# A bounce through memory issued on another queue, and weight loads put behind a cast, in an attention and Fourier-mix kernel on one core

## The chip, the cores and the metric

The kernel runs on one core of one Trainium2 chip. A core has a matrix engine (TensorE, PE in the profile; PEld is its loading of weights), a vector engine (VectorE, DVE), a scalar engine (ScalarE, ACT), GpSimd (POOL), a synchronisation engine (SyncE, SP) that here only issues transfers, and 16 DMA engines. Each engine works through its own list of instructions in order, and a transfer is issued by an instruction in the list of SP, ACT or POOL. The metric is the device time of one execution in microseconds (us); lower is better.

## The reference

Batch 4, 8 heads, 768 positions, head size 64. Attention keeps a local band of 96 positions and the first 8 positions, with a linear distance bias; its output goes through a two-dimensional Fourier transform, and a two-layer block with a residual follows.

```python
scores = scale * np.matmul(q, k.transpose(0, 1, 3, 2))
scores = scores + bias[None, :, :, :]
scores = np.where(keep, scores, -1000000000.0)      # band of 96, and the first 8
a = softmax(scores);  x = heads_joined(a @ v)        # 4 x 768 x 512
mixed = np.real(np.fft.fft(np.fft.fft(x, axis=1), axis=2))
u = x + mixed
un = (u - mu) / np.sqrt(var + 1e-06)
out = u + np.maximum(un @ w_ch1, 0.0) @ w_ch2        # 512 -> 2048 -> 512
```

## The kernel before

Each batch b goes through the same stages. Loads of q, k, v for one pair of heads at a time (hp 0 to 3) come in on SP (`run_dma`, L365; `load`, L320). They are cast to 16 bits (`cast_qk`, L369 on ACT and L373 on POOL; v in `cast_v0`, L414 on POOL), transposed (`trans`, pt, L515, copied to qkT by L521 on DVE or L525 on ACT), and multiplied to scores (`score`, sc, L542 to L552). ACT takes the exponential into ex (L575). A few global columns go their own way (`glob`, pgl and eg; `v_global`, pvg and vG). `v_place` (pvp, L427) puts v into its place. `av` (pav, L669 and L680) multiplies by v, and DVE divides the result into X, the tile x of a batch (L699, L700).

X is then used twice. DVE folds it (L797 to L819), PE makes the first Fourier stage y (py, L881, copied to zy by L896 on ACT and L898 on DVE) and, with mirrored copies made on POOL (L916 to L929), the second one (`u_unit`, pu, L961). Beside that, `bounce(b)` (L709) writes X to a scratch tensor xd in memory (L719) and reads it back into xr in the other order of rows that the Fourier output has (L727). `u_unit` adds the two on DVE: u = pu + xr (L980). From there come the normalised un (L995 on ACT, L997 on DVE), its transpose ptu and unT (L1025, L1033, L1035), the sum of squares (L1004), the hidden layer ph (L1053, 8 units for each of the 12 pieces c of 256 rows, three pieces to a batch; evacuated to hT by L1059 on ACT or L1060 on DVE), and the output layer pg (L1076), whose result is added to u (L1085) and stored (L1090).

The two weight matrices are 4 MB each in 32 bits. `wload` (L1159) loads and casts them in eight transfers, four of w_ch1 (L1164) and four of w_ch2 (L1169), all issued by POOL. They go into the buffers that staged q and k of batch 1. `hold` (L1178), a tiny transfer on SP, waits for the last of them; it is the gate (`("gate",)`) behind which the loads of batch 2 stand.

The order on every engine is fixed when the program is built. A planner (class `Plan`) keeps a clock for each engine and for the DMA, and gives each piece of work to the engine and place where it would end first by its estimates; `later` (L61) registers a piece with its needs, its cost on the engine and, as `dma=`, the time its transfer takes. So a changed need or cost can move many other instructions.

For batch 0 the bounce writes two halves, heads 0 to 3 and heads 4 to 7, as four transfers of 192 KB on SP; for the other batches it writes two of 384 KB on ACT. The transfers issued by SP and ACT signal their end on eight semaphores, DMAHW0 to DMAHW7, taken in turn in the program's order, and an issue that takes one again waits until the earlier transfer on it has landed.

Of the kernel before, what the change touches and what calls it, by code (L numbers as in the profile page):

```python
# [176 lines left out]
def kernel(  # L177
# [11 lines left out]
    nc = tc.nc  # L189
# [94 lines left out]
    def free(tag, i):  # L284
        i -= NBUF[tag]
        return [("free", tag, i)] if i >= 0 else []

    def buf(tag, i, shape, dtype, users):
        pl.users(("free", tag, i), users)
        return wk.tile(shape, dtype, tag=tag, name=f"{tag}_{i}", bufs=NBUF[tag])  # L290
# [417 lines left out]

    def bounce(b):  # L709

        on, eng = ("ACT", nc.scalar) if b else ("SP", nc.sync)
        parts = ((0, 256), (256, 512)) if b == 0 else ((0, Dm),)
        for n, (c0, c1) in enumerate(parts):
            def wr(n=n, c0=c0, c1=c1):
                if n == 0:
                    XD[b] = dr.tile([S, Dm], FP16, tag="xd", name=f"xd_{b}", bufs=2)
                rows = XD[b][:, c0:c1].rearrange("(j m t) d -> t m j d", t=2, m=64)
                for t in range(2):
                    eng.dma_start(rows[t], X[b][64 * t:64 * t + 64, :, c0:c1])  # L719
            pl.later([(on, 1.2, wr)], [("x", b, hp, jp) for hp in range(c0 // P, c1 // P) for jp in range(NP)]  # L720
                     + [("xw", b, n - 1)] * (n > 0), 0.0, [("xw", b, n)], [("free",) + XT[b]] * (3 - len(parts)),
                     lat=1.7, dma=2.4 / len(parts))

        def rd():
            XR[b] = buf("xr", b, [P, NS, Dm], FP16, 3)
            rows = XD[b].rearrange("(m r) d -> m r d", r=6)
            eng.dma_start(XR[b], rows)  # L727
        pl.later([(on, 0.5, rd)], [("xw", b, n) for n in range(len(parts))] + free("xr", b), 0.0, [("xr", b)], lat=1.7, dma=3.8 if b else 2.4)
# [369 lines left out]
    with tc.manual_schedule():  # L1098
# [60 lines left out]
        def wload(i):  # L1159
            a = i % 4  # L1160
            if i < 4:
                if i == 0:
                    W1[0] = buf("w1", 1, [P, ND, 4 * Dm], FP16, 1)
                nc.gpsimd.dma_start(W1[0][:, :, a * 512:(a + 1) * 512],  # L1164
                                    moe_w_ch1[:, a * 512:(a + 1) * 512].rearrange("(c p) f -> p c f", p=P))
            else:
                if i == 4:
                    W2[0] = buf("w2", 1, [P, NJ, Dm], FP16, 1)
                nc.gpsimd.dma_start(W2[0][:, 4 * a:4 * a + 4, :],  # L1169
                                    moe_w_ch2[a * 512:(a + 1) * 512, :].rearrange("(c p) f -> p c f", p=P))  # L1170
        for i in range(8):
            needs = [("ld", 7, 1), ("free", "w1", 0)] if i == 0 else [("wl", 3), ("free", "w2", 0)] if i == 4 else [("wl", i - 1)]
            pl.later([("POOL", 0.85, lambda i=i: wload(i))], needs, 0.0,
                     [("w1" if i < 4 else "w2", i % 4)], lat=2.2, dma=3.3, rank=0,
                     then=lambda t, i=i: pl.tok.__setitem__(("wl", i), pl.t["POOL"]))
# [4 lines left out]
        for b in range(B):  # L1180
# [36 lines left out]
            else:  # L1217
# [12 lines left out]
                for half in range(2):  # L1230
                    for jp in range(NP):
                        av(b, (2 * half, 2 * half + 1), jp)
            bounce(b)
            if b < DB:
                fold_3(b)
# [53 lines left out]
```

## Time and profile before

| | before |
|---|---|
| time, median of 3 runs | 287.69 us (286.93 to 289.57) |
| the profiled execution: own time, span in the profile | 288.64 us, 286.9 us |
| PE busy | 258.0 us, 90% |
| PE weight loads, DVE, ACT, POOL busy | 173.3, 153.9, 150.1, 55.9 us |
| mean granted clock of PE, share of full speed | 0.969 |
| queue of SP | 31.40 MB, 44.8% of 16 engines' span |
| queue of POOL (the weights) | 4.19 MB, 8.7% |
| queue of ACT | 4.72 MB, 6.6% |

The profile is one execution. Busy shares are means over the span. The profile's chain of the work that ended last lists what the last instruction goes back to; the waits name, for each engine, whose result it waited for. A transfer's time to landing runs from the start of its issue to its last byte.

### The profile page before, as it was taken

To read this page: it belongs to the slowest core of one execution; us is meant where nothing else is said; L and a number is where in the kernel's file an instruction comes from. 1 tells how busy PE (TensorE), PEld (TensorE's weight loads), DVE (VectorE), ACT (ScalarE), POOL (GpSimd) and SP (SyncE) were. 2 spreads that over 40 slices of the span, in tenths; PEclk is the share of its full clock that TensorE was granted. 3 is DMA by queue.
4 is the path that set the end of the run, shared out by engine and by line. 5 is a ranking of instruction groups with operands and counts; after the bars stand their busy time and mean duration, and the time that the engine had idled before them with its cause. 6 is when DMAs were issued, how large, how long until landed. Compare 5 with 4: busy or idle time off the path is not lost.

```text
span 286.9 us, 6013 instructions
## 1 busy us (share of the span) xinstructions
PE 258.0 (90%) x2448; PEld 173.3 (60%) x2448; DVE 153.9 (54%) x323; ACT 150.1 (52%) x256; POOL 55.9 (19%) x126
## 2 busy tenths in 40 slices
PE   1898994048999999999999999999999999999994
PEld 1354574017778785578558466677677567777441
DVE  4557930057039952669268969666995552211121
ACT  1489772028875962578684144979044155534000
POOL 1442496001121042130311024201002211100000
PEclk9999999557999999999999999999999999999999
DMA  7999999997005895795696897400073020100211
GB/s 218 289 292 315 317 239 217 223 228 169 3 10 158 156 250 114 199 224 125 125 235 161 162 248 180 94 13 2 2 172 124 37 75 1 39 37 0 75 73 73
DMA packets 70301, 40.69 MB, mean 142 GB/s; under 512 B 27394, under 2 KB 66306, under 8 KB 70274
## 3 DMA queue, kind: packets, MB, share of 16 engines
q1 hardware_dynamic: 63218, 31.40, 44.8%
q0 software_dynamic: 4224, 4.19, 8.7%
q10 hardware_dynamic: 2832, 4.72, 6.6%
q8 instruction: 19, 0.31, 0.5%
q14 instruction: 8, 0.07, 0.1%
HBM read 31.92 MB, written 9.44 MB: 144 GB/s over the span
## 4 chain that ended last, share of the span: by engine, by line
PE 69%; SPq 2%; POOL 1%; DMA 1%; DVE 1%; issue 1%; DVEq 0%; POOLq 0%
PE ph L1053 29%; PE pg L1076 26%; PE py L881 3%; PE pav L680 3%; PE sc L552 3%; PE pu L961 2%; PE ptu L1025 2%; SPq L494 1%; PE pav L669 1%; DMA out_dram<-u 1%; POOL ww L929 1%; PE pgl L632 1%; DVE u L980 0%; SPq L336 0%; POOL v L454 0%
## 5 line engine op out<-in xcount | busy, mean ns | idle before, releaser
L1053 PE MATMUL ph<-unT,w 128*128 128x256 f16 x768 | 93.7, 273 | 0.5 <-ACT v L444 0.5
L1076 PE MATMUL pg<-w,hT 128*128 128x512 f16 x384 | 89.3, 379 | 0.0
L1053 PEld LDWEIGHTS <-w 128*128 128x128 f16 x768 | 72.5, 98 | 16.4 <-issue 4.7
L1059 ACT ACTIVATE hT<-ph 128x512 f16<-128x512 f32 x76 | 45.3, 596 | 44.9 <-PE ph L1053 44.4
L1076 PEld LDWEIGHTS <-hT 128*128 128x128 f16 x384 | 36.8, 98 | 37.1 <-issue 0.4
L1085 DVE SCALAR_TENSOR_TENSOR u<-pg,sm,u 128x512 f32<-128x512 f32 x24 | 18.0, 748 | 45.7 <-PE pg L1076 45.5
L980 DVE SCALAR_TENSOR_TENSOR u<-pu,xr 128x512 f32<-128x512 f32 x24 | 15.6, 686 | 22.2 <-DMA xr<-xd 15.3
L575 ACT ACTIVATE ex<-sc 128x992 f16<-128x992 f32 (+2 forms) x24 | 21.1, 926 | 10.2 <-PE sc L552 9.9
L572 ACT ACTIVATE er<-sc 128x992 f16<-128x992 f32 (+2 forms) x24 | 21.7, 922 | 6.1 <-PE sc L552 5.2
L995 ACT ACTIVATE un<-u,sm 128x512 f16<-128x512 f32 x10 | 7.2, 719 | 27.0 <-DVE sm L984 27.0
L1060 DVE TENSOR_SCALAR hT<-ph 128x512 f16<-128x512 f32 x20 | 13.8, 691 | 10.2 <-PE ph L1053 10.0
L542 PE MATMUL sc<-dist,sid 128*128 128x480 f16 x16 | 5.4, 426 | 15.0 <-DVE u L980 15.0
L929 POOL COPY ww<-zy 128x512 f16<-128x512 f16 x16 | 9.4, 614 | 44.9 <-PE py L881 44.9
L552 PE MATMUL sc<-qkT 64*128 64x256 f16 (+1 forms) x192 | 17.5, 269 | 0.5 <-DVE qkT L521 0.5
L1011 POOL TENSOR_SCALAR sm<-sm 128x2 f32<-128x2 f32 x12 | 2.3, 193 | 75.8 <-ACT un L1004 75.6
L680 PE MATMUL pav<-v,ex 128*128 128x65 f16 x352 | 16.2, 193 | 0.7 <-DVE x L700 0.7
L1035 DVE COPY unT<-ptu 128x1024 f16<-128x1024 f16 x10 | 6.9, 688 | 17.7 <-PE ph L1053 15.0
L680 PEld LDWEIGHTS <-ex 128*128 128x128 f16 x352 | 15.0, 97 | 2.0 <-DVE x L700 0.9
L896 ACT ACTIVATE zy<-py 128x1024 f16<-128x1024 f32 (+1 forms) x10 | 8.6, 856 | 14.2 <-PE py L881 14.1
L587 DVE TENSOR_TENSOR ex<-er,mk 128x992 f16<-128x992 f16 (+2 forms) x24 | 15.0, 641 | 1.7 <-ACT er L572 1.7
L369 ACT ACTIVATE qk<-qs 128x384 f16<-128x384 f32 (+1 forms) x29 | 13.6, 526 | 4.6 <-DMA qkT<-qk 4.6
L1004 ACT ACTIVATE un<-un 128x512 f16<-128x512 f16 x24 | 14.8, 621 | 1.6 <-PE ptu L1025 1.6
(102 smaller groups left out, 304.3 us busy)
## 6 DMA issues: line engine op xcount, KB each, us to landing
out_dram<-u SPq DMA_DIRECT2D x24, 256.0 KB, 2.1
w<-in_moe_w_ch_dram POOLq DMA_DIRECT2D x8, 512.0 KB, 16.2
qs<-in_q_dram SPq DMA_DIRECT2D x9, 384.0 KB, 4.1
qs<-in_k_dram SPq DMA_DIRECT2D x9, 384.0 KB, 4.3
u<-in_v_dram SPq DMA_DIRECT2D x8, 384.0 KB, 7.1
qs<-in_v_dram SPq DMA_DIRECT2D x16, 192.0 KB, 3.9
xr<-xd ACTq DMA_DIRECT2D x3, 768.0 KB, 5.0
w<-in_q_dram SPq DMA_DIRECT2D x4, 384.0 KB, 7.1
```

The source lines that it names most:

```text
L552: nc.tensor.matmul(pa[:, s, c0:c0 + cw], TT[n][lo:lo + 64, 1, i * P:(i + 1) * P], TT[n][lo:lo + 64, 0, i * P:i * P + cw], start=(b > 1), s ...
L572: A(mine(), cut(pa), AF.Exp, 0.0, 0.125)
L575: A(cut(expst[hp][:, :, g * 512:g * 512 + (384 if g == 2 else 512)]), cut(pa), AF.Exp, 0.0, 0.125)
L587: VT(o, mine(), m, op=ALU.mult)
L680: nc.tensor.matmul(po[:, jj, hh * 65:(hh + 1) * 65], lhsT, v16[b % 2][:, i, h, 0:65], start=(jp == 0 and a == 0), stop=(a == len(ops) - 1) ...
L980: V.scalar_tensor_tensor(u[:, a].rearrange("p (n r) -> p n r", r=4), pu[:, a].rearrange("p (r n) -> p n r", r=4), 1.0, XR[b][:, rr].rearra ...
L1004: A(x, x, AF.Square, accum_out=MV[c][:, a, 2:3])
L1053: nc.tensor.matmul(ph[:, a * CH:(a + 1) * CH], W1[0][:, d, jb * P:(jb + 1) * P], UNT[c][:, d, :], start=(d == 0), stop=(d == ND - 1))
L1059: pl.later([("ACT", act(512), lambda: A(dst, ph, AF.Relu)), ("DVE", dve(512), lambda: V.tensor_scalar_max(dst, ph, 0.0))], [], e, [("h", c ...
L1060: ("DVE", dve(512), lambda: V.tensor_scalar_max(dst, ph, 0.0))],
L1076: nc.tensor.matmul(pg, HT[c][:, jb, t * P:(t + 1) * P], W2[0][:, jb, :], start=(jb == 0), stop=(jb == NJ - 1))
L1085: V.scalar_tensor_tensor(UT[c][:, t, :], pg, MV[c][:, t, 3:4], UT[c][:, t, :], op0=ALU.mult, op1=ALU.add)
```

## The change

Two edits, and an estimate that goes with the first. The bounce of batch 0 is issued in ACT's list, writes and read, where it stood in SP's. The planner's estimate for each of its two writes goes from 1.2 to 2.6 us. The first weight load needs ("vc", 5), the cast of v of batch 1's second pair of heads on POOL, where it needed the landing of the last k of batch 1, ("ld", 7, 1).

```diff
     def bounce(b):
-        on, eng = ("ACT", nc.scalar) if b else ("SP", nc.sync)
+        on, eng = "ACT", nc.scalar
         parts = ((0, 256), (256, 512)) if b == 0 else ((0, Dm),)
...
-                     lat=1.7, dma=2.4 / len(parts))
+                     lat=1.7, dma=2.4 if b else 2.6)
...
         for i in range(8):
-            needs = [("ld", 7, 1), ("free", "w1", 0)] if i == 0 else [("wl", 3), ("free", "w2", 0)] if i == 4 else [("wl", i - 1)]
+            needs = [("vc", 5), ("free", "w1", 0)] if i == 0 else [("wl", 3), ("free", "w2", 0)] if i == 4 else [("wl", i - 1)]
```

The planner then orders anew. ACT's list of before, from the place where the first half of X of batch 0 is done (ex_81 and ex_78 are exponentials, qk_455 to qk_669 casts of batch 1's q and k, qkT_678 a transpose's copy):

```order
L444 ACTIVATE v_82<-pvp_442 128x3x2x64 [waits PE_49]
L369 ACTIVATE qk_455<-w_0_163 128x768 [waits DMAHW0_49]
L575 ACTIVATE ex_81<-sc_0_461 128x2x496 [waits PE_49]
L369 ACTIVATE qk_498<-w_0_163 128x768 [waits DMAHW1_49,Activation_49,Pool_49]
L575 ACTIVATE ex_81<-sc_1_474 128x2x2x240 [waits PE_49]
L575 ACTIVATE ex_81<-sc_2_485 128x2x384 [waits PE_49]
L645 ACTIVATE eg<-pgl_1_501,gb 32x512 [waits PE_49]
L369 ACTIVATE qk_581<-w_0_215 128x768 [waits DMAHW4_49,PE_49,Activation_49]
L575 ACTIVATE ex_78<-sc_0_597 128x2x496 [waits PE_49]
L575 ACTIVATE ex_78<-sc_1_610 128x2x2x240 [waits PE_49]
```

The same place after:

```order
L444 ACTIVATE v_82<-pvp_442 128x3x2x64 [waits PE_49]
L719 DMA xd_471<-x_368 64x6x256 [waits DVE_49]
L719 DMA xd_471<-x_368 64x6x256 [waits DMAHW1_49]
L575 ACTIVATE ex_81<-sc_0_461 128x2x496 [waits PE_49]
L575 ACTIVATE ex_81<-sc_1_474 128x2x2x240 [waits PE_49]
L575 ACTIVATE ex_81<-sc_2_485 128x2x384 [waits PE_49]
L645 ACTIVATE eg<-pgl_1_502,gb 32x512 [waits PE_49]
L369 ACTIVATE qk_591<-w_0_215 128x768 [waits PE_49,DMAHW4_49,Activation_49,Pool_49]
L575 ACTIVATE ex_78<-sc_0_597 128x2x496 [waits PE_49]
L719 DMA xd_471<-x_368 64x6x256 [waits DMAHW0_49,DVE_49]
L719 DMA xd_471<-x_368 64x6x256 [waits DMAHW1_49]
L575 ACTIVATE ex_78<-sc_1_627 128x2x2x240 [waits PE_49]
```

The four writes now stand between exponentials, three of them behind a semaphore of an earlier transfer, and two casts have left this stretch of ACT for POOL; the read L727 follows seven rows later, behind the last exponential into ex_79 and ahead of the first copy of y, and one more cast and the copy qkT_678 have left ACT by then, the copy for DVE.

POOL's list of before, from the third transpose of batch 1 (kG are small copies, er casts of v of batch 1):

```order
L481 COPY kG_85<-qkT_646 64x8 x2
L1164 DMA w_1_689<-in_moe_w_ch_dram 128x4x512
L481 COPY kG_85<-qkT_678 64x8
L1164 DMA w_1_689<-in_moe_w_ch_dram 128x4x512
L481 COPY kG_85<-qkT_678 64x8
L1164 DMA w_1_689<-in_moe_w_ch_dram 128x4x512 x2
L414 CAST er_755<-u_257 128x768
L1169 DMA w_1_760<-in_moe_w_ch_dram 128x4x512
L414 CAST er_762<-u_271 128x768
L1169 DMA w_1_760<-in_moe_w_ch_dram 128x4x512 x3
```

The same place after:

```order
L481 COPY kG_85<-qkT_645 64x8 x2
L373 CAST qk_668<-w_0_215 128x768
L481 COPY kG_85<-qkT_685 64x8 x2
L414 CAST er_732<-u_257 128x768
L414 CAST er_763<-u_271 128x768
L1164 DMA w_1_765<-in_moe_w_ch_dram 128x4x512 x4
L929 COPY ww_818<-zy_759 128x512
L1169 DMA w_1_833<-in_moe_w_ch_dram 128x4x512
L916 COPY rev_0_853<-zy_759 128x2
L917 COPY rev_0_853<-zy_759 128x2x127
L918 COPY rev_0_853<-zy_759 128x256
L1169 DMA w_1_833<-in_moe_w_ch_dram 128x4x512
```

All eight weight loads now come behind both casts, and the four of w_ch2 stand between the mirrored copies of batch 0.

ACT's list of before, ahead of the first hidden unit (hT from ph_0; ex_81 is batch 1's last pair of heads here):

```order
L1004 ACTIVATE un_917,sm_888<-un_917 128x512 x2
L1059 ACTIVATE hT_1017<-ph_0_1022 128x512
L609 ACTIVATE vG_87<-pvg_0_1050 32x4x64 x2
L1059 ACTIVATE hT_1017<-ph_1_1059 128x512
L1059 ACTIVATE hT_1017<-ph_2_1070 128x512
L645 ACTIVATE eg<-pgl_0_1080,gb 64x512
L1059 ACTIVATE hT_1017<-ph_3_1086 128x512
L1059 ACTIVATE hT_1017<-ph_4_1096 128x512
L575 ACTIVATE ex_81<-sc_0_1106 128x2x496
```

The same place after:

```order
L575 ACTIVATE ex_81<-sc_0_961 128x2x496
L575 ACTIVATE ex_81<-sc_1_983 128x2x2x240
L575 ACTIVATE ex_81<-sc_2_994 128x2x384
L444 ACTIVATE v_83<-pvp_1003 128x3x2x64
L1004 ACTIVATE un_953,sm_901<-un_953 128x512 x2
L645 ACTIVATE eg<-pgl_0_1039,gb 64x512
L609 ACTIVATE vG_87<-pvg_0_1050 32x4x64
L995 ACTIVATE un_1079<-u_1044,sm_1045 128x512
L609 ACTIVATE vG_87<-pvg_0_1050 32x4x64
L1059 ACTIVATE hT_1102<-ph_0_1107 128x512
```

Batch 1's last three exponentials, eg and vG, which stood between hidden units, now come ahead of the first of them; on PE the scores, pgl, pvg and two pav units move with them.

## Rows read from the trace of the kernel before

**Rows 1.** The page: PE's busy tenths in 40 slices of 7.17 us.
```profile
PE   1898994048999999999999999999999999999994
```
**Rows 2.** The waits of PE: total us, times, longest.
```profile
PE sc L542 <- DVE u L980: 15.0, 1, 15.0
```
**Rows 3.** Timeline of DVE: start, us, instruction, idle before it and its releaser.
```profile
22.93 0.69 DVE L700 TENSOR_TENSOR x<-pav,rc 128x512 f16<-128x512 f32 x1
...
30.86 0.42 DVE L700 TENSOR_TENSOR x<-pav,rc 128x256 f16<-128x256 f32 x1
...
60.25 0.69 DVE L980 SCALAR_TENSOR_TENSOR u<-pu,xr 128x512 f32<-128x512 f32 x1 [15.31 <-DMA xr<-xd]
```
**Rows 4.** Timeline of SP's list.
```profile
17.65 2.24 SPq L365 DMA_DIRECT2D w<-in_q_dram  x1
...
25.65 0.43 SPq L365 DMA_DIRECT2D w<-in_q_dram  x1
...
35.41 3.96 SPq L719 DMA_DIRECT2D xd<-x  x4
53.38 0.35 SPq L727 DMA_DIRECT2D xr<-xd  x1
65.67 0.32 SPq L1178 DMA_DIRECT2D hold<-w  x1
```
**Rows 5.** Issues: KB each, median us to landing; the third row of 38 to 39.5 us alone.
```profile
w<-in_q_dram SPq DMA_DIRECT2D x4, 384.0 KB, 7.1
...
xr<-xd SPq DMA_DIRECT2D x1, 768.0 KB, 6.7
...
xd<-x SPq DMA_DIRECT2D x2, 192.0 KB, 13.5
...
xd<-x ACTq DMA_DIRECT2D x4, 384.0 KB, 4.6
...
xr<-xd ACTq DMA_DIRECT2D x3, 768.0 KB, 5.0
```
**Rows 6.** Queues from 46 to 50 us: packets, MB, share of 16 engines.
```profile
q0 software_dynamic: 573, 0.57, 83.7%
q1 hardware_dynamic: 572, 0.28, 34.9%
```
**Rows 7.** Timeline of POOL.
```profile
34.84 0.95 POOL L1164 DMA_DIRECT2D w<-in_moe_w_ch_dram  x1
...
40.14 0.83 POOL L414 CAST er<-u 128x768 f16<-128x768 f32 x1
```
**Rows 8.** Timelines of ACT, its exponentials and its issues, and of PE's first pu.
```profile
36.47 3.45 ACT L575 ACTIVATE ex<-sc 128x992 f16<-128x992 f32 x4
...
89.36 1.34 ACTq L719 DMA_DIRECT2D xd<-hT  x2
...
44.07 1.06 PE L961 MATMUL pu<-t,zy 128*128 128x128 f16 x16
```
**Rows 9.** Stretches: length, busy us (instructions) of PE, PEld, DVE, ACT, POOL, clock, DMA share, GB/s.
```profile
60.25:70.57 10.32, 8.07 (x92) 5.19 (x93) 8.74 (x24) 6.77 (x13) 0.92 (x2) 0.63 0.84 174
...
61.61:67.90 6.29, 6.29 (x61) 3.67 (x62) 4.78 (x13) 4.71 (x9) 0.36 (x2) 0.50 0.60 113
...
70.57:117.90 47.33, 47.33 (x450) 34.43 (x449) 24.38 (x48) 30.89 (x57) 8.86 (x20) 1.00 0.55 118
118.14:282.96 164.82, 164.72 (x1424) 110.50 (x1424) 93.57 (x182) 82.04 (x147) 21.59 (x53) 1.00 0.42 103
```
**Rows 10.** The six stretches, 72.05 to 85.94 us, of batch 1's scores, pvg, pgl and two pav.
```profile
sum 4.01, PE 4.01 PEld 1.99 DVE 0.99 ACT 3.34 POOL 0.42; mean PE 0.67 PEld 0.33 DVE 0.17 ACT 0.56 POOL 0.07
```
**Rows 11.** Groups of ACT from 61.7 to 83.4 us: busy, mean ns, idle before.
```profile
L575 ACT ACTIVATE ex<-sc 128x960 f16<-128x960 f32 (+2 forms) x5 | 4.5, 909 | 1.1 <-PE sc L552 0.9
...
L609 ACT ACTIVATE vG<-pvg 32x256 f16<-32x256 f32 x2 | 0.7, 374 | 0.1
L645 ACT ACTIVATE eg<-pgl,gb 64x512 f16<-64x512 f32 x1 | 0.7, 683 | 0.0
```

## The prediction

> **What bounds the kernel now.** I read the slices of the page first. PE is busy nearly all through, but for the start and for three slices near 50 to 65 us, the 0 among them [rows 1]. The waits give that hole one cause: PE stands 15.0 us, once, for the addition u on DVE [rows 2]. DVE's timeline carries it on: u had been idle 15.31 us and was released by the landing of xr, at 60.25 us [rows 3]. So the hole is the bounce of batch 0, and SP's timeline shows where the bounce loses its time. The first half of X is complete when L700 ends at 22.93 + 0.69 = 23.62 us and the second at 31.28 [rows 3], but SP issues the four writes from 35.41 on, behind its loads, 11.8 us after the first half is there, and the read only at 53.38 [rows 4]. The last writes took 13.5 us to land [rows 5], because POOL had begun to issue the weights at 34.84 [rows 7]: between 46 and 50 us the weights' queue and SP's moved the same number of packets, 573 and 572, but the weights' are twice as large and hold 83.7% of the engines' time [rows 6]. From 70.57 us to the last matmul at 282.96, PE is busy all the time except 0.33 us [rows 9] (0.23 between the two stretches, 0.10 in the second). So whatever brings the first hidden unit ph_0 forward brings the end forward by as much, until PE finds a new wait.
>
> A second loss hangs on the hole: when PE resumes, the granted clock is 0.50, the 1.2 GHz level, for 6.29 us of full work [rows 9]. That is up to 3.1 us, but DVE is busy 8.74 of the 10.32 us of that stage too, so I don't take it as a gain of its own.
>
> **The change, part by part.** I follow the time of four events: the read's landing, u, ph_0, the end.
>
> *Bounce on ACT.* Its first write goes out at 23.7. A pair of write issues costs ACT 1.34 us [rows 8], and the second write waits for DMAHW1, which in the program's order is the load issued at 17.65; a load lands 7.1 us after its issue [rows 5], so 24.8. ACT is free again at 25.5 to 25.7, and what is queued behind it, the exponential that before began at 24.36, is 1.3 us late. Two casts that stood in this stretch are now POOL's, so the following eg is only 0.6 late, and X's second half is done at 31.9 instead of 31.28. The second pair waits for the load issued at 25.65, which lands at 32.75, and say 33.3 since the first writes share its engines. ACT is free at 33.3 + 1.34 = 34.65; the exponential behind it is 2.9 late. A cast and a qkT copy have left the list before the read (0.84 and 1.44, given back), and three exponentials at 3.45 / 4 = 0.86 us each [rows 8] lead up to it, so ACT comes to the read at about 39.7, against 39.05 for the same place before. For the landing of the writes I take ACT's other ones, 4.6 us [rows 5], not SP's 13.5, since no weight is under way: 34.65 + 4.6 = 39.3. So ACT hardly waits. The read takes 5.0 us (ACT's) to 6.7 us (SP's, beside the weights) [rows 5]: it lands at 44.8 to 46.7.
>
> *What ACT's lateness costs.* The late exponentials free their PSUM banks later, so y starts some 1.5 us later, and pu_0, which ended at 45.1 (44.07 + 1.06 [rows 8]), ends near 46.6. This is my estimate from the 2.9 us less what is given back; bounds 0 and 3 us. u therefore starts at **46.8**, where both come together, against 60.25. Bounds: 45.1 (no lateness at all) and 50.5 (the second writes land in 8.8 us, half way between the two rows).
>
> *From u to ph_0.* Before, this took 10.32 us with ACT busy 6.77 [rows 9]. After, more stands ahead of ph_0: three exponentials, eg and two vG copies are new and one exponential has moved out, 2 x 0.909 + 0.683 + 0.748 = 3.25 us [rows 11], which makes 10.0 us for ACT, the busiest engine (DVE 8.74 + 0.99 [rows 9, 10]). un starts some 1.5 us after u, and about 1 us of waits between ACT, PE and DVE will remain, about what L575 alone waited before, 1.1 [rows 11]. Together 12.5 us: ph_0 at **59.3**. Bounds 11 and 14.
>
> *From ph_0 to the end.* Before, 282.96 - 70.57 = 212.39 us, less 0.33 idle. The scores, pvg, pgl and two pav that stand ahead of ph_0 now are 4.01 us of PE [rows 10]. Left are 208.05. PE then ends at 267.4, and the tail after the last matmul, 286.9 - 282.96 = 3.94, is untouched: 271.3.
>
> *Weights later.* The first is issued behind the cast er of the second pair. That ran at 40.14 before, after weight issues [rows 7]; now its v load, delayed by the writes that share the engines, sets it, and I take the same 40.1 and 0.83 us. The first issue moves from 34.84 to about 41.0, 6.2 us. From the first issue to hold, which waits for the last weight, it was 65.67 - 34.84 = 30.8 us [rows 4, 7], beside 0.79 MB of writes, 0.79 MB of read and the end of the loads. After, the first writes are gone from it, but batch 1's writes come into it. So hold goes at 71.8. PE wants the last quarter of w_ch1 seven units into the hidden layer, near 66, and half of 30.8 puts it at 56.4. It wants the last quarter of w_ch2 near 76, 4 us after hold. ACT wants the first q of batch 2, behind the gate, near 77, when that has just landed. What hides the delay is thus the stage from u to ph_0 and nine units of work; the cover is 4 us for pg and about none for the cast. For that wait, and for batch 1's writes beside the last weights, I add 1.0 us, bounds 0 and 4.
>
> Sum: 271.3 + 1.0 = 272.3 of span, 14.6 less than 286.9. The profiled execution took 288.64 us, 1.74 outside its span, and the median of the runs is 287.69, 0.95 lower; taking the same 14.6 off the median gives **273.1**.
>
> Against this change speaks the Trainium skill, DMA: Bandwidth & Descriptors, section "Issuing engines are not separate DMA queues": transfers run on the same 16 engines whoever issues them, and another issuer saves only the issuer's time, usually small. By that rule the edit of the queue would be worth next to nothing, the last rival below. The trace disagrees on "small" for this list (the 11.8 us above) and agrees that no bytes are saved, the first rival.
>
> **Rivals.**
> *The wait moves to the weights.* The bytes are the same, so what the bounce no longer waits, the weights do. If hold comes at 77 instead of 71.8, pg of the first piece and the cast of batch 2's q, both in order on engines that PE needs, stand 4 to 5 us: 278. For it: batch 1's writes now fall into the last weights. Against: the 30.8 us already held as many foreign bytes.
>
> *The bounce is still slow.* The second writes land in 13.5 us as SP's did: 48.2. ACT stands at the read from 39.7 with the copies of y behind it, PE stops, the read lands at 55, u starts 8.5 us later than I say and the clock falls as before (up to 3): 283. For it: the loads fill the engines until about 40. Against: ACT's writes of other batches, 4.6.
>
> *Slower than before.* The gate alone could do that. It must hold batch 2's first q 14.6 us longer than I say, hold at 86 or later, so the weights would need 45 us instead of 30.8; decisive from there on. Nothing in the trace slows them so: with the bounce beside them they held 83.7% [rows 6].
>
> *It doesn't do what it says.* If PE, freed at 46.8, lacked work until weights came, 13 us would be lost again: no change. Against: ten us of ACT and nine of PE work stand ahead of ph_0, and w_ch1's first quarter needs only a quarter of 15.4 us after 41.
>
> **How the numbers follow.** My sum 0.70, with its own range 269.5 to 276.5; the weights 0.17; the slow bounce 0.08; no change 0.02; slower 0.03. Low end: u at 45.1, 11 us to ph_0, no wait: 45.1 + 11 + 208.05 + 3.94 = 268.1, which is 268.9 on the median; all at once is unlikely, so 269.5. High end: 50.5, 12.5, waits of 3 give 278.0, which is 278.8; with the weights' 278 inside I close at 279.5. A measurement tells about 1% (2.9 us) from no change. Faster by over 1%: 0.70 + 0.17 + 0.08 = 0.95; same 0.02; slower 0.03.
>
> **What would show it.** Right: the writes on ACT's queue from about 24 and 33 us; the read landing by 47; no PE wait of over 3 us near 50, and a granted clock at 2.4 GHz throughout; ph_0 near 59; hold near 72; PE without gaps after it. Wrong: an ACT wait of several us at L727 before 48 (slow bounce); PE waiting at pg for w, or ACT at L369 for qs, near 75 (weights); ph_0 later than 62 with ACT idle in between (my 12.5 is off).

## Result, and the profile after

The changed kernel takes **279.8 us** (median of 4 runs, 278.83 to 280.46), the kernel before beside it 288.32 (286.93 to 289.57): a ratio of 0.970 (95% interval 0.9645 to 0.9761). The gain is 8.5 us; the prediction said 14.6 and a range up to 279.5. One further run of the same kernel gave 278.78 us and a further series of four 279.03, both below. The profiled execution took 280.46 us, the longest of its four; its span is 278.7. The ratios, but not the medians and ranges, leave out slow runs, those over 1.5% longer than the fastest of their kernel, such as the 283.47 us further down.

From the page, PE's busy tenths and its clock in 40 slices, where [rows 1] had the hole:

```profile
PE   1999789598789999999999999999999999999994
PEclk9999999999999999999999999999999999999999
```

The waits of PE (total us, times, longest). The 15.0 us for u of [rows 2] are gone. The longest behind the start are now one for un and two for hT:

```profile
PE ptu L1025 <- ACT un L995: 2.5, 1, 2.5
PE ph L1053 <- DVE hT L1060: 2.2, 2, 1.4
```

Timelines of the engines (start, us, instruction, idle before it), for the rows that answer to [rows 3, 4, 7]:

```profile
25.99 0.69 DVE L700 TENSOR_TENSOR x<-pav,rc 128x512 f16<-128x512 f32 x1
...
26.71 1.88 ACTq L719 DMA_DIRECT2D xd<-x  x2
...
34.98 1.26 ACTq L719 DMA_DIRECT2D xd<-x  x2
...
41.61 0.35 ACTq L727 DMA_DIRECT2D xr<-xd  x1
...
42.67 3.19 POOL L1164 DMA_DIRECT2D w<-in_moe_w_ch_dram  x4
...
49.81 0.69 DVE L980 SCALAR_TENSOR_TENSOR u<-pu,xr 128x512 f32<-128x512 f32 x1 [0.29 <-PE pu L961]
...
51.16 2.78 DVE L984 TENSOR_SCALAR sm<-sm 128x2 f32<-128x2 f32 x1
...
53.98 0.72 ACT L995 ACTIVATE un<-u,sm 128x512 f16<-128x512 f32 x1 [3.05 <-DVE v L443]
...
64.33 1.03 PE L1053 MATMUL ph<-unT,w 128*128 128x256 f16 x8
...
69.54 0.31 SPq L1178 DMA_DIRECT2D hold<-w  x1
```

The issues (KB each, median us to landing), against [rows 5]:

```profile
xd<-x ACTq DMA_DIRECT2D x4, 192.0 KB, 6.4
xr<-xd ACTq DMA_DIRECT2D x1, 768.0 KB, 4.3
```

The two stretches from u to ph_0 and behind it (columns as in [rows 9]):

```profile
49.81:64.33 14.52, 10.35 (x186) 6.86 (x179) 12.88 (x28) 11.19 (x23) 9.29 (x18) 1.00 1.24 206
64.33:118.00 53.67, 51.05 (x465) 37.81 (x462) 29.68 (x59) 29.78 (x58) 11.30 (x23) 1.00 0.74 164
```

The bounce goes as the change says. In this profile u no longer waits for xr at all: the read landed at 41.61 + 4.3 = 45.9, and u waited for pu. Yet u comes at 49.81 instead of 46.8, ph_0 14.52 us later instead of 12.5, and from ph_0 to the end it is 278.7 - 64.33 = 214.4 us instead of 213.0. In this last stretch PE has 53.67 - 51.05 = 2.62 us of idle instead of 1.0; its work and the tail together came out 0.2 us shorter. These three terms make the span 3.0 + 2.0 + 1.4 = 6.4 us longer than the 272.3 predicted. The experiments ask where each comes from.

### The profile page after: what moved, and what is told of

Same layout as the page of the kernel before. It is cut to its first block, busy times and chain, and to the rows that moved or that the text cites. A ratio compares the mean times of both kernels' runs of the same rounds, so it can differ in the third digit from the quotient of the medians.

```text
span 278.7 us, 6005 instructions
## 1 busy us (share of the span) xinstructions
PE 258.7 (93%) x2448; PEld 173.2 (62%) x2448; DVE 157.9 (57%) x323; ACT 148.0 (53%) x255; POOL 60.8 (22%) x127
## 2 busy tenths in 40 slices
DMA packets 70301, 40.69 MB, mean 146 GB/s; under 512 B 27394, under 2 KB 66306, under 8 KB 70274
## 3 DMA queue, kind: packets, MB, share of 16 engines
q10 hardware_dynamic: 4576, 6.29, 8.3%
## 4 chain that ended last, share of the span: by engine, by line
PE 81%; DVE 8%; ACT 4%; issue 2%; DMA 2%; POOL 1%; ACTq 1%; SPq 0%; DVEq 0%; POOLq 0%
PE pg L1076 29%; PE ph L1053 29%; PE py L881 5%; PE sc L552 4%; PE pav L680 3%; PE pu L961 3%; ACT ex L575 2%; PE pt L515 2%; DVE qkT L521 2%; PE ptu L1025 2%; DMA ident<-idm 2%; PE sc L547 2%; PE pav L669 1%; PE sc L542 1%; DVE sm L984 1%
## 5 line engine op out<-in xcount | busy, mean ns | idle before, releaser
L1059 ACT ACTIVATE hT<-ph 128x512 f16<-128x512 f32 x73 | 43.6, 597 | 48.1 <-PE ph L1053 46.9
L1060 DVE TENSOR_SCALAR hT<-ph 128x512 f16<-128x512 f32 x23 | 15.9, 690 | 11.5 <-PE ph L1053 11.5
L1011 POOL TENSOR_SCALAR sm<-sm 128x2 f32<-128x2 f32 x12 | 3.2, 264 | 71.9 <-ACT un L1004 71.7
L980 DVE SCALAR_TENSOR_TENSOR u<-pu,xr 128x512 f32<-128x512 f32 x24 | 15.6, 688 | 4.7 <-PE pu L961 4.0
L369 ACT ACTIVATE qk<-qs 128x384 f16<-128x384 f32 (+1 forms) x31 | 14.5, 528 | 6.1 <-DMA qkT<-qk 4.8
L995 ACT ACTIVATE un<-u,sm 128x512 f16<-128x512 f32 x12 | 8.5, 716 | 16.1 <-DVE sm L984 13.0
L552 PEld LDWEIGHTS <-qkT 64*128 64x128 f16 x192 | 6.0, 96 | 16.1 <-issue 13.2
L896 ACT ACTIVATE zy<-py 128x512 f16<-128x512 f32 (+1 forms) x10 | 8.1, 810 | 14.7 <-PE py L881 14.7
L898 DVE CAST zy<-py 128x512 f16<-128x512 f32 (+1 forms) x9 | 8.3, 927 | 10.5 <-ACT zy L896 6.4
```

The lines of the kernel that those rows point to most:

```text
L552: nc.tensor.matmul(pa[:, s, c0:c0 + cw], TT[n][lo:lo + 64, 1, i * P:(i + 1) * P], TT[n][lo:lo + 64, 0, i * P:i * P + cw], start=(b > 1), s ...
L980: V.scalar_tensor_tensor(u[:, a].rearrange("p (n r) -> p n r", r=4), pu[:, a].rearrange("p (r n) -> p n r", r=4), 1.0, XR[b][:, rr].rearra ...
L1059: pl.later([("ACT", act(512), lambda: A(dst, ph, AF.Relu)), ("DVE", dve(512), lambda: V.tensor_scalar_max(dst, ph, 0.0))], [], e, [("h", c ...
L1060: ("DVE", dve(512), lambda: V.tensor_scalar_max(dst, ph, 0.0))],
```

## Experiments

**Both kernels once more.** No edit.

> The kernel before once more, for a second profile of its start. Theory (the start varies by itself): PE's slow first matmuls last a different time from run to run, so the third L700, which ended at 23.62 us in the first profile, may end anywhere from 23 to 27 us, and the end does not follow it, since the addition u waits for the read anyway and starts at 60 us within 0.5. Rival (the start is fixed by the program, and the change moved it): it ends at 23.6 within 0.3 again.

> The changed kernel once more. Theory (the start varies by itself, and nothing hides it any more): the third L700 ends between 23 and 27 us, and u starts 23.1 us after that end, as in its first profile (49.81 after 26.68), so an early start is an early end. DVE's L984 at u takes over 2 us again, in a stretch where POOL is busy without a gap. Rival: L700 ends at 26.7 within 0.3 again.

Measured: 287.11 and 278.78 us, spans 285.3 and 277.0. The start of a run varies. Before, the first half of X was ready at 23.62 [rows 3]; in the second profile of the same kernel at 26.23, 2.6 us later, and it costs nothing, because DVE's idle time ahead of u shrinks from 15.31 to 11.16 us. u itself came 1.7 us earlier (I had said within 0.5), as the read was issued earlier, at 51.70 instead of 53.38:

```profile
25.54 0.69 DVE L700 TENSOR_TENSOR x<-pav,rc 128x512 f16<-128x512 f32 x1
...
58.55 0.69 DVE L980 SCALAR_TENSOR_TENSOR u<-pu,xr 128x512 f32<-128x512 f32 x1 [11.16 <-DMA xr<-xd]
```

The changed kernel's second profile had the early start (24.12 against 26.68 in the first), and u still came at 49.65, so my expectation of 23.1 us from the one to the other was wrong, as was the long L984: it took 0.17 us. DVE's, POOL's and ACT's timelines:

```profile
23.43 0.69 DVE L700 TENSOR_TENSOR x<-pav,rc 128x512 f16<-128x512 f32 x1
...
39.82 3.18 POOL L1164 DMA_DIRECT2D w<-in_moe_w_ch_dram  x4
...
41.61 0.35 ACTq L727 DMA_DIRECT2D xr<-xd  x1
...
49.65 0.69 DVE L980 SCALAR_TENSOR_TENSOR u<-pu,xr 128x512 f32<-128x512 f32 x1 [2.98 <-POOL ww L929]
...
50.99 0.17 DVE L984 TENSOR_SCALAR sm<-sm 128x2 f32<-128x2 f32 x1
```

and the read's landing, from its issues:

```profile
xr<-xd ACTq DMA_DIRECT2D x1, 768.0 KB, 7.8
```

pu_0 was done at 46.9 here. The row names POOL as the releaser, but the read issued at 41.61 with 7.8 us to landing arrives at 49.4, just ahead of u, and I take that to be what u waited for. The early start brought POOL to the weights at 39.82, ahead of the read; in the late start they came at 42.67, behind it, and the read took 4.3. So in these two profiles a late start delays pu, an early one is followed by a slower read, and u comes at nearly the same time. The wait for u has a price behind it: PE stands 3.0 us, and from u to ph_0 the granted clock is 0.87, where the first profile had 1.00 (columns as in [rows 9]):

```profile
49.65:62.66 13.01, 10.45 (x157) 7.78 (x157) 10.82 (x28) 10.26 (x21) 6.54 (x12) 0.87 1.23 203
```

**One edit at a time.** The bounce on ACT with the weights' need as before, and the reverse:

```diff
  bounce_only = changed kernel, but in wload's needs
-            needs = [("vc", 5), ("free", "w1", 0)] if i == 0 else ...
+            needs = [("ld", 7, 1), ("free", "w1", 0)] if i == 0 else ...
  weights_only = kernel before, but
-            needs = [("ld", 7, 1), ("free", "w1", 0)] if i == 0 else ...
+            needs = [("vc", 5), ("free", "w1", 0)] if i == 0 else ...
```

> The bounce on ACT, the weights where they were before. Theory (weights beside the writes are what makes the bounce slow): the second half's writes, issued near 35 us, land only after 9 to 13 us, ACT stands at the read for several us, the read lands at 50 to 54, u starts there, and the time is 282 to 286 us. Rival (the issuing list was all): u waits for nothing but pu, and the time is that of the whole change, 279.8.

> The weights behind the cast, the bounce still on SP behind the loads. Theory: SP issues the writes from 35 to 39 us, they land in 5 to 7 us as no weight is under way until 41 to 42, the read goes out at 44 to 46 and lands 5 to 7 us later beside the weights, u starts near 51, 2 us later than with the whole change, and the time is 281 to 284 us. Rival (the issuing list was all): u starts near 60 and the time is that of before, 288.

Measured: the bounce alone 278.49 us (277.91 to 283.47), ratio 0.966 (0.962 to 0.971); the weights alone 284.19 (283.86 to 285.23), ratio 0.988 (0.983 to 0.993); the kernel before beside them 287.8. The first edit alone brings the whole gain. My expectation that early weights would hold up ACT's writes and read was wrong. In the bounce alone the weights are issued from 35.36 on, the second writes still land in 6.5 us and the read in 7.0, at 47.9, ahead of pu:

```profile
33.55 1.26 ACTq L719 DMA_DIRECT2D xd<-x  x2
...
35.36 0.95 POOL L1164 DMA_DIRECT2D w<-in_moe_w_ch_dram  x1
...
48.59 0.69 DVE L980 SCALAR_TENSOR_TENSOR u<-pu,xr 128x512 f32<-128x512 f32 x1 [0.29 <-PE pu L961]
...
57.57 1.92 PE L1053 MATMUL ph<-unT,w 128*128 128x256 f16 x16
```

With the weights alone the bounce stays in SP's list, but loses most of its slowness: from the first write's issue at 35.57 to u it takes 15.6 us, where it took 60.25 - 35.41 = 24.8 [rows 3, 4]. Of the 9.1 us by which u comes earlier, the span keeps 286.9 - 282.1 = 4.8: the stage from u to ph_0 takes 15.95 us instead of 10.32, at a granted clock of 0.79.

```profile
35.57 3.47 SPq L719 DMA_DIRECT2D xd<-x  x4
...
42.27 0.35 SPq L727 DMA_DIRECT2D xr<-xd  x1
...
51.13 0.69 DVE L980 SCALAR_TENSOR_TENSOR u<-pu,xr 128x512 f32<-128x512 f32 x1 [6.48 <-DMA xr<-xd]
```

and the stretch from u to ph_0 (columns as in [rows 9]):

```profile
51.13:67.08 15.95, 12.59 (x164) 7.75 (x165) 11.33 (x31) 11.33 (x21) 1.84 (x5) 0.79 1.06 177
```

The 9.3 us of the one and the 3.6 of the other don't add up to the 8.5 of both. My reading, which no run isolates, is that each takes the writes out of the weights' way, and once that is done the other has nothing left to remove.

**The start.** Nine matmuls on zeros ahead of the program, so that PE should be at work before its first operands land, in the kernel before and in the changed one:

```diff
+        wt = bank("xx", "pwarm")
+        for i in range(9):
+            nc.tensor.matmul(wt[:, i % 2, :], EG[:, 0:128], EG, start=True, stop=True)
         pl.run([...])
```

> The changed kernel with nine matmuls of 512 columns on zeros put ahead of PE's first own work, while it waits for the first transfer; they add nothing to the output. Theory (PE's slow start is now on the path): PE runs at its fast pace from about 6 to 9 us, the third L700 ends at 22 to 23.5, and the time falls by 1 to 4 us to 276 to 278.8. Rival (the start is set by the loads, not by PE's pace): L700 ends where it did and the time stays at 279.8 within 0.7.

> The kernel before with the same nine matmuls. Theory (there the hole hides the start): L700 ends earlier as well, but u still starts at 60 us within 0.7, since writes, weights and read are set by SP's list and the DMA engines, and the time stays at 288.3 within 0.8. Rival (the start counts in both): it falls by as much as the changed kernel's does.

Measured: 278.88 us (278.4 to 280.99) for the changed kernel with it, 287.59 (284.16 to 292.3) for the one before: no difference that these runs can tell. In both profiles the first twelve transposes are fast (0.84 us, else 1.46), but that need not last. In the changed kernel's profile (first half of X at 26.38, a late start in spite of it) PE then waits for ACT and POOL, busy 1.16 of 3 us, and behind that the granted clock is 0.50, the 1.2 GHz level:

```profile
10.00:13.00 3.00, 1.16 (x24) 0.85 (x13) 1.25 (x3) 1.32 (x3) 1.52 (x2) 0.95 1.21 287
13.00:16.70 3.70, 3.52 (x25) 0.95 (x25) 1.48 (x3) 1.53 (x3) 1.58 (x5) 0.50 1.23 292
```

So this didn't take the late start away, where I had said 22 to 23.5 us, and what an always early start would be worth was not measured directly. With the late start u came at 49.51, as above. In the kernel before, the profile with the nine matmuls had an early start (23.75).

**The weights of the second layer early.** In the changed kernel POOL's list between y and un mixes mirrored copies, casts and the four issues of w_ch2 (the change's rows of POOL). Here all four stand right behind w_ch1:

```diff
         def wload(i):
...
-            else:
-                if i == 4:
-                    W2[0] = buf("w2", 1, [P, NJ, Dm], FP16, 1)
-                nc.gpsimd.dma_start(W2[0][:, 4 * a:4 * a + 4, :], ...)
+            if i == 3:
+                W2[0] = buf("w2", 1, [P, NJ, Dm], FP16, 1)
+                for a in range(4):
+                    nc.gpsimd.dma_start(W2[0][:, 4 * a:4 * a + 4, :], ...)
```

> The changed kernel with the four loads of w_ch2 issued right behind the four of w_ch1; every other engine's order is as in the changed kernel. Theory (POOL's unbroken work from 49.5 to 55.6 us, issues between copies, holds DVE off at L984): L984 takes under 1 us, the stretch from u to the first hidden unit shrinks from 14.5 to 12 to 13 us, and the time falls by 1.5 to 2.5 us to 277.3 to 278.3. Rival (the copies alone hold DVE, not the issues): L984 still takes over 2 us and the time stays at 279.8 within 0.7.

> Both edits on the changed kernel, the early w_ch2 issues and the nine matmuls. Theory: the two gains are in different stretches and add, 2.5 to 6 us, 273.8 to 277.3. Rival (one of them is caught by a later wait): the time is that of the better one alone.

Measured: 277.39 us (275.82 to 277.75), and with the nine matmuls 277.61 (276.6 to 278.32), so the two don't add. The profile of the former is of its fastest run, 275.82, where the other four took 277.34 to 277.75. It is nearly the prediction's: u at 46.84 (46.8 was said), ph_0 at 59.62 (59.3), span 274.0 (272.3). Timelines of POOL, DVE and PE:

```profile
46.84 0.69 DVE L980 SCALAR_TENSOR_TENSOR u<-pu,xr 128x512 f32<-128x512 f32 x1 [0.29 <-PE pu L961]
...
47.88 1.60 POOL L414 CAST er<-u 128x768 f16<-128x768 f32 x2
...
48.18 0.55 DVE L984 TENSOR_SCALAR sm<-sm 128x2 f32<-128x2 f32 x1
...
59.62 1.03 PE L1053 MATMUL ph<-unT,w 128*128 128x256 f16 x8
```

With the nine matmuls (which here left the first transposes at 1.43 us), the read was issued at 40.46, just ahead of the weights (40.69), and took 4.3 us. But the tiny L984 took 2.19, so ph_0 came at 62.18:

```profile
48.68 1.63 POOL L414 CAST er<-u 128x768 f16<-128x768 f32 x2
48.70 2.19 DVE L984 TENSOR_SCALAR sm<-sm 128x2 f32<-128x2 f32 x1
...
50.22 0.64 POOL L929 COPY ww<-zy 128x512 f16<-128x512 f16 x1
```

L984 works on 128x2 elements and mostly takes 0.17 us. Here it ends at 50.89, POOL's copy at 50.86. No weight issue stands in this stretch of POOL, so my theory that it takes issues between the copies was wrong. In all profiles where the first L984 is long, its end lies within 0.05 us of the end of a POOL instruction: 53.94 and 53.92 in the changed kernel's first, 48.73 and 48.71 in w2_early (the first of its two casts takes 0.83). I read this as DVE standing there until POOL lets it go. POOL's row for the changed kernel's first profile:

```profile
53.08 0.84 POOL L414 CAST er<-u 128x768 f16<-128x768 f32 x1
```

**Taking L984 off DVE.** One row moves, for the first u only; then, in a second kernel, the second half of un too; and the first together with the early weights. The changed kernel was timed beside them.

```diff
-                V.tensor_scalar_mul(sm[:, :, 1], sm[:, :, 0], -SC / Dm)
+                (V.tensor_scalar_mul if c else nc.scalar.mul)(sm[:, :, 1], sm[:, :, 0], -SC / Dm)
  sm_un_act: and
-                pl.later([("ACT", 0.52, ...), ("DVE", 0.38, ...)],
+                pl.later([("ACT", 0.52, ...), ("DVE", 0.38, ...)][:2 if c else 1],
```

> The changed kernel unaltered, timed for a third time beside the three kernels that follow. From its first two profiles: u starts at 49.6 to 49.8 whether the first loads and scores run early or late, since an early start only leads to a read that shares the engines with the weights (issued 39.8 against 41.6). So the median should be 278.5 to 280.5 as before, and the profile has u near 49.7, ph_0 at 62.7 (L984 short) or 64.3 (L984 long). If instead the late start alone set the time, a profile with the third L700 ending near 24 would have u near 47 and a span of 275.

> The changed kernel with one row moved: the scaling of 128x2 elements behind the first u (L984, DVE) is done by ACT, for this one u only. Theory (DVE cannot start an operation that reads and writes SBUF only while POOL is at its own copies and casts; operations that read PSUM are not held): L984 on ACT takes 0.2 to 0.3 us, and the cast L443 behind it on DVE runs in its usual 0.55; but the next SBUF operation on DVE, the second half of un at L997 (0.48), meets the same POOL work and is held up to 2 us in its place, so that PE still waits for un, and u to ph_0 stays 13.0 to 14.5; 278 to 280. Rival (the row itself is at fault, or its place behind the accumulator's read): nothing else is held, un is complete 1.5 to 2.5 us earlier in every run, u to ph_0 is 12.5, and the median is 277 to 278.

> The kernel of the run before this one with the second half of the first un on ACT too, so that between u and ptu no operation of DVE reads and writes SBUF only. Theory of the hold: no DVE row between u and un above its usual length, PE waits less than 1 us at ptu, u to ph_0 12.5 to 13.5 in any run (one more un, 0.72 us, on ACT): 277.5 to 279, 1 us under the unaltered kernel. Rival (POOL's lateness, not the hold, is what PE waits for: v, kG and ww come late anyway): u to ph_0 stays 14.5, no gain.

> The second weight matrix issued right behind the first (so that POOL's run of copies and casts has no weight issues in it), together with the scaling L984 of the first u on ACT. The profile of the former alone came out close to the prediction's own steps: u 46.8, ph_0 59.6, span 274.0. Theory of the hold: its bad runs are those in which L984 is held by POOL's two casts (2.2 us in one profile, 0.55 in another), so with L984 on ACT the median is 276 to 277 and the highest under 278. Rival (its spread comes from the start and the read alone): 277.4 as measured without the move of L984.

Measured, the four in turn: 279.03 us (278.47 to 280.04), **277.47** (277.06 to 277.65), 278.4 (277.16 to 279.4) and 278.44 (277.23 to 279.94). With the one row moved the kernel is 1.6 us faster, and the four runs of the two kernels don't overlap. But the two other kernels with L984 on ACT overlap with the unaltered one, and the 1.6 us are not shown to be the price of the held row. The changed kernel's profile had the long L984 again (2.78), and 14.52 us from u to ph_0; with L984 on ACT it is 61.41 - 48.00 = 13.41:

```profile
49.35 0.21 ACT L984 ACTIVATE sm<-sm 128x2 f32<-128x2 f32 x1 [2.98 <-DVE u L980]
...
50.44 0.68 DVE L997 TENSOR_SCALAR un<-u,sm 128x512 f16<-128x512 f32 x1
...
61.41 1.03 PE L1053 MATMUL ph<-unT,w 128*128 128x256 f16 x8
```

Of the 2.6 us between these two spans, 1.1 lie in this stage and 1.4 in u, which came earlier after an early start. Against the unaltered kernel's second profile, with an early start and a short L984 too, the span is 1.3 us shorter, and there the gain lies in u alone (48.00 against 49.65); the stage is 0.4 longer.

The half of my theory by which the next operation of DVE on SBUF would be held up to 2 us in its place is wrong: L997 took 0.68 instead of 0.48 beside a cast of POOL (49.99 to 50.83). The rival has the median right (277 to 278) but not the stage, for which it said 12.5. The two other kernels bring nothing on top, and for the second of them I had said 276 to 277: their stages from u to ph_0 are 13.43 and 12.78 us, and u comes at 48.30 and 48.33, held by reads of 7.1 and 7.2 us behind the weights.

All profiles of the changed order side by side (us; "released by" is what u waited for last, the read where its landing is the later one, also in two rows where the profile names another; "clock" is the granted clock from u to ph_0):

| kernel | first half of X ready | read, first weight issued | read takes | u, released by | L984 | u to ph_0 | clock | span |
|---|---|---|---|---|---|---|---|---|
| changed, 1st | 26.68 | 41.61, 42.67 | 4.3 | 49.81, pu | 2.78 | 14.52 | 1.00 | 278.7 |
| changed, 2nd | 24.12 | 41.61, 39.82 | 7.8 | 49.65, read | 0.17 | 13.01 | 0.87 | 277.0 |
| changed, 3rd | 26.28 | 41.14, 42.26 | 4.2 | 49.40, pu | 2.78 | 14.52 | 1.00 | 278.3 |
| warm_after | 26.38 | 40.99, 42.36 | 4.3 | 49.51, pu | 2.77 | 15.35 | 0.89 | 279.2 |
| w2_early | 23.99 | 40.50, 39.69 | 6.1 | 46.84, pu | 0.55 | 12.78 | 1.00 | 274.0 |
| warm_w2 | 23.42 | 40.46, 40.69 | 4.3 | 47.35, pu | 2.19 | 14.83 | 0.88 | 276.5 |
| sm_act | 23.64 | 40.74, 39.59 | 7.1 | 48.00, read | on ACT | 13.41 | 0.87 | 275.7 |
| sm_un_act | 23.60 | 40.97, 39.59 | 7.1 | 48.30, read | on ACT | 13.43 | 0.87 | 276.1 |
| w2_sm | 24.15 | 40.90, 39.85 | 7.2 | 48.33, read | on ACT | 12.78 | 1.00 | 275.4 |

In each of them the span is 214.3 to 214.4 us longer than ph_0's start.

## Why the prediction was right and wrong

**Right: what the hole was, and that it goes.** PE's 15.0 us for u are gone, and the bounce alone brings the whole gain. In the first profile the clock is 1.00 from u on, where [rows 9] had 0.50 for 6.29 us. My sign of being right, "a granted clock at 2.4 GHz throughout", was not met everywhere: PE still stood 3.0 us for u in the second profile, and from u to ph_0 the clock is 0.87 to 0.89 in five of the nine profiles. The rule that I weighed against it (the Trainium skill, DMA: Bandwidth & Descriptors, section "Issuing engines are not separate DMA queues") would have made that edit worth next to nothing; the measured 9.3 us decide. What was saved begins with time in the issuer's list, as the rule says: with the bounce alone the writes go out at 24.02 and 33.55 us, not from 35.41 on. It wasn't small.

**Right: the weights.** hold was said for 71.8 and went at 69.54 (64.4 to 68.6 in the other profiles with either edit). Luck had a part in the number: the first weight went out 1.7 us later than I said, at 42.67, and from there to hold took 26.9 us instead of 30.8. PE never waits for w, and ACT has no wait for qs near 75. The rival "The wait moves to the weights" was not seen. ACT's lateness of 1.5 us at pu was right too: in the first profile pu_0 ends 4.6 us later than before, 3.06 of it from the first half of X.

**Wrong, 3.0 us: u at 46.8.** Two inputs of this step failed. X's first half at 23.62 was taken from one profile as if it were fixed. It lay between 23.4 and 26.7 in the profiles taken here; before, the hole swallowed the difference, and after, nothing does when pu comes last. The other is the landing of the last writes in 4.6 and of the read in 5.0 to 6.7: the writes took 5.6 to 7.7, so the read was issued at 40.5 to 41.6 instead of 39.7, and in five of the six early starts of the table the weights' issue, which I had put behind it at 41.0, came ahead of it at 39.6 to 39.9. The read then took 6.1 to 7.8, otherwise 4.2 to 4.3. With an early start and a read of 6.1 us, u came at 46.84, so the sum of the step was sound and its inputs were not. My bounds, 45.1 and 50.5, held every value (half way between 4.6 and 13.5 is 9.05, not the 8.8 that I wrote, which moves the upper one little).

**Wrong, 2.0 us: 12.5 us from u to ph_0.** It is 12.8 to 13.4 us where L984 is short or on ACT, and 14.5 to 15.4 where L984 is held, beyond my bound of 14. The clock goes with the rest of the spread: 12.8 are the two at 1.00, 13.0 to 13.4 the three at 0.87; held, it is 14.52 at 1.00 and 15.35 at 0.89. ACT is busy 11.19 us in the first profile's stage, where I had summed 10.0. I had counted ACT and DVE by the busy time of the kernel before, where POOL was busy 0.92 of 10.32 us in this stage [rows 9]; after, it is busy 9.29 of 14.52. I saw the rows of POOL move into this stage and put what they do to DVE at nothing. What the hold costs is best seen in the unaltered kernel itself: 14.52 us from u to ph_0 in the two profiles with L984 at 2.78, 13.01 in the one at 0.17, which is 1.5 us although the clock was lower in the latter (u also came later against POOL's rows there). The 1.6 us of sm_act are of this size, but its spans differ in u as well. That POOL's work holds the row is read from the ends of the rows, as that work itself was not taken away. The Trainium skill, SBUF — State Buffer, section "SBUF: two separate sides", says that GpSimd and DVE share a pair of ports, that a GpSimd operation and a DVE operation in a two-port mode (or one with two inputs in SBUF, against a GpSimd operation that reads SBUF) lock it against each other, and that the one that starts second stands for the whole instruction of the first. The trace agrees that the held row ends with a POOL instruction; but the 2.78 us reach over four instructions of POOL, L997 was hardly held, and in the second profile L984 took 0.17 us beside a weight issue on POOL (50.98 to 51.72). No run here shows the mode of these rows. Which end releases DVE, and why one row is held and another not, stays open.

**Wrong, 1.4 us: 1.0 us of later waits.** I looked for them at the gate and at the last weights, where there were none. Two waits of PE for hT, 1.40 and 0.78 us, took their place. They stand in every profile of the changed order, and in those of each edit alone. Together with smaller ones PE idles 2.62 us between 64.33 and 118, and no run tried to remove them; their cause stays open.

The miss is thus one of sizes in three terms that all went the same way, and my range had no room for it: its high end took u at 50.5 and waits of 3 us, but 12.5 for the stage from u to ph_0, not that stage's own bound of 14. None of the rivals happened whole; "The bounce is still slow" did in part, as ACT stood at the read (idle 2.66 us in the second profile, put down there to the row behind the read) and u waited for it, for 3 us rather than 8.5.

**The best version measured** is sm_act: 277.47 us, 1.6 less than the changed kernel in the same series. w2_early, 277.39 in another series without the changed kernel, is as good as far as these runs tell.

## What to carry to other kernels

A wait that is removed uncovers what it hid: before trusting a time that lies ahead of it, look at a second profile, since variation that cost nothing there can reach the end afterwards. When a change moves work of POOL, check DVE's small operations in the new place too, not only POOL's own list. And where two engines issue transfers at nearly the same time, price both orders, because which one goes first can change from run to run.

## What the runs showed of the hardware

**PE's speed at the start.** The changed kernel's first and second profiles run the same pair of matmuls at different speeds (the same line and place in the program, 480 columns each), while the granted clock reads 1.00 from 10 to 20 us in both:

```profile
16.32 0.98 PE L542 MATMUL sc<-dist,sid 128*128 128x480 f16 x2
```

```profile
14.75 0.58 PE L542 MATMUL sc<-dist,sid 128*128 128x480 f16 x2
```

Until about 18 us the first profile's matmuls run at the lower speed; in the second nearly all run at the higher one from 10 us on, and the same pair comes 1.6 us earlier. The column of the granted clock doesn't show this; the row's duration does.

**The order of two issues.** The 768 KB read of batch 0 took 4.2 to 4.3 us to land in the four profiles in which it was issued 0.2 to 1.4 us ahead of the first weight load, and 6.1 to 8.7 in the seven with either edit in which that load went first, even by 0.8 us (the 8.7 is the read on SP with the weights alone). No run moved the order by itself; three of the four fast reads followed a late start.
